# Products with v in eight 64x32 streams, maxima exchanged by ScalarE in some slots, and new tables of steps

## The chip, the cores and the metric

The kernel runs on one core of one Trainium2 chip. The metric is the time of one execution on the device, in microseconds (us), and the time given for a kernel is the median of several runs. One execution is also recorded by the hardware profiler; its trace gives the start, length and waits of single instructions.

## The reference

The reference computes a thresholded attention and then a SwiGLU block on its output. There are 8 batches, 8 heads, 576 positions and 64 values per head; the second part sees 4608 tokens of 512 values and has 1536 hidden values. All is float32.

```python
scores = scale * np.matmul(q, k.transpose(0, 1, 3, 2))
thresh = np.max(scores, axis=-1, keepdims=True) - tau
scores = np.where(scores >= thresh, scores, -1000000000.0)
scores = scores - np.max(scores, axis=-1, keepdims=True)
attn = np.exp(scores)
attn = attn / (np.sum(attn, axis=-1, keepdims=True) + 1e-09)
attn_out = np.matmul(attn, v)
x = attn_out.transpose(0, 2, 1, 3).reshape(B * S, H * D)
g = x @ w_gate
out = (g * (1.0 / (1.0 + np.exp(-g))) * (x @ w_val)) @ w_out
```

## The kernel before, in words

**Two streams of work on one TensorE.** The attention of one batch is computed while the SwiGLU block of the batch before it runs, so that TensorE always has matmuls. Batch 0's attention comes first and is written in another form (until about 142 us of the span); the text here is about what follows. Batches 1 to 7 each have four segments (one segment is a pair of heads), and each segment has five *slots*. A slot takes 128 query positions of both heads, or, in the fifth slot of a segment, the last 64. Within a batch the slots are numbered kk = 0 to 19; kk = 4, 9, 14 and 19 are the short fifth slots. Over the first two of these batches the code also counts s = 20 x (batch - 1) + kk, from 0 to 39. After batch 7 (about 1198 us) the attention is over, and only the rest of the SwiGLU block runs.

**What a slot does.** `slot_scores` (matmul on L1513) computes one or two *units* of scores. A unit is eight matmuls of shape 64x32 (64 rows of contraction, 32 output partitions), each streaming 288 columns, into a PSUM tile `sc`. There are two such tiles, used in turn, so a unit can start only when the masks of the unit before last have been computed. Then `slot_rest` makes the jobs of the other engines, in this chain:

1. VectorE takes each row's maximum, negated (L1535, tile `mx`). A query's row lies in two groups of 32 partitions, so the maxima of neighbouring groups are exchanged: `largest` does that by four small VectorE reductions across groups (L1541) and a final one (L1542, tile `nm`).
2. ScalarE computes the threshold (L1545, tile `th`) and the exponentials from PSUM into `pall` (L1549).
3. VectorE applies the mask and sums (L1550). This frees the PSUM tile.
4. ScalarE exchanges the sums of the two groups by four small copies (L1564), VectorE adds them and takes the reciprocal (L1569, L1570).
5. Each of the two or four tiles of the slot is scaled by the reciprocal: the odd tiles by GpSimd (L1577) unless the slot is in the table `BY_ACT`, the others by ScalarE (L1580). The short slots are scaled by ScalarE always.
6. VectorE transposes the slot's tiles in blocks of 32x32 (L1581).

**The products with v.** `attend` (L1600) takes a whole segment, once the transposes of all its five slots are done. It runs directly behind the scores of the second slot of the next segment (kk = 1, 6, 11, 16; the last of the 28 segments follows other work). Nine steps over blocks of keys accumulate in two PSUM banks, one for each half of the contraction rows; before the change a step is four matmuls of shape 64x64, each streaming 288 columns.

**What fills the rest of a slot on TensorE.** `block_part` puts matmuls of the SwiGLU block behind the scores. For batch 0's tokens (while batch 1's attention runs) these are plain products (`plain_group`, L1037), as many steps per slot as the table `PLAIN` says, and then output products (L1103) as `CH0` says. From batch 2's attention on they are products by a seven-product scheme with the gate and value weights (`Group`, L937; PSUM tiles `pa`, `pb`, `pe`), with steps per slot in `GV` for kk = 2 to 14; and then the products with the output weights, in one such level for the second batch of tokens (`Outputs`, L1103, table `CH`), in two levels from then on (`Deep`, L1305 and L1317, table `CD`). `CH` holds for kk = 16 to 19 and for kk = 0 and 1 of the next batch. A step of `GV` is one product of 1.73 us.

**What sets the order.** The engines run their instructions in the order in which they are written. A planner (`Plan`) chooses that order while the program is made: every job has an engine, an expected time, a rank and the jobs that it needs, and the planner simulates the engines' queues with these times. `pe(took, fn, ...)` is a TensorE step: it forces the jobs that it needs, runs the other engines' jobs up to the present planned time, and adds `took`. So the times written in the code change no instruction, but they change which of two jobs comes first on an engine.

```python
m = pe(0.655, fn, *ready, *deps, *deep_jobs[o])       # L1308, one inner product of the two-level scheme
marks.append(pe(0.7, fn, *deps, *seg["qk"]))          # L1516, one unit of scores
m = pe(4.75, fn, *seg["turned"], seg["vj"], *holds[0].deps, *holds[1].deps)   # L1603, products with v
slot_rest(seg, t, pss, marks, b > DEEP and kk in BY_ACT)   # L1766, DEEP is 2
```

By the last of these lines, batches 1 and 2 (b at most `DEEP`) scale all their odd tiles on GpSimd, and `BY_ACT` counts for batches 3 to 7 alone.

Of the kernel before, what the change touches and what calls it, by code (L numbers as in the profile page):

```python
# [14 lines left out]
ALU = mybir.AluOpType  # L15
AX = mybir.AxisListType
# [11 lines left out]
class Plan:  # L28
# [68 lines left out]
    def pe(self, took, fn, *deps):  # L97
        self.force(*deps)
        for d in deps:
            if d is not None:  # L100
                self.t = max(self.t, (d.end if isinstance(d, Job) else d) + self.HOP)
        self.run(self.t)
        fn()
        self.t += took
        return self.t + self.PIPE
# [7 lines left out]
def kernel(  # L113
# [11 lines left out]
    nc = tc.nc  # L125
    P = 128
    B, H, S, D = q.shape
# [4 lines left out]
    G = 32  # L132
    NG = P // G
# [3 lines left out]
    NK = NJ // 2  # L137
    SM = 512
    NT = SM // P
    SH = S // 2  # L140
# [421 lines left out]
    ready = deque()  # L562
# [161 lines left out]
    job, pe = plan.job, plan.pe  # L724
# [57 lines left out]
    DEEP = 2  # L782
# [422 lines left out]
    deep_jobs = [[] for _ in operands]  # L1205
# [27 lines left out]
    class Deep:  # L1233
# [60 lines left out]
        def nested(self, o, holds, first, *deps):  # L1294

            ws = weights_of(o)
            begun = set() if first else {0, 1}
            for n in self.ORDER:
                a, ready = self.inner[o][n]
                bank_, at_ = self.AT[n]  # L1300

                def fn(n=n, a=a, bank_=bank_, at_=at_):
                    ps = holds[bank_].ap()[:, at_ * P:(at_ + 1) * P]
                    for f in range(NF2 // 2):
                        nc.tensor.matmul(ps, a[:, f, :], ws[n][:, f, :], start=bank_ not in begun, stop=True, skip_group_check=True)  # L1305
                        begun.add(bank_)

                m = pe(0.655, fn, *ready, *deps, *deep_jobs[o])  # L1308
            return m

        def flat(self, o, a, hold, first, *deps):
# [206 lines left out]

    turned_jobs = {}

    def slot_rest(seg, t, pss, marks, by_act=False):
        m = 2 * len(pss)
        mx, nm, th, ri, tot = statistics("mx", "nm", "th", "ri", "tot")
        sm = sums[0]
        sums.rotate(1)
        old_sums, sum_users[0] = sum_users[0], []
        sum_users.rotate(-1)
        scs = [ps[:, h, 0:SH] for ps in pss for h in range(2)]
        base, order = seg["p"]
        first = order(t)  # L1530
        ps = [pall[:, base + (first + x) * SH:base + (first + x + 1) * SH] for x in range(m)]
        whole = pall[:, base + first * SH:base + (first + m) * SH]
        rs = []
        for x, tile_ in enumerate(pss):
            rs.append(job("DVE", 0.72, lambda x=x, tile_=tile_: nc.vector.tensor_reduce(  # L1535
                out=mx[:, 2 * x:2 * x + 2, 0], in_=tile_[:, :, 0:SH], axis=AX.X, op=ALU.max, negate=True), marks[x], rank=0))

        def largest():
            for g in range(NG):
                o = g ^ 1  # L1540
                nc.vector.tensor_reduce(out=mx[g * G:(g + 1) * G, 0:m, 1], in_=mx[o * G:(o + 1) * G, 0:m, 0:1], axis=AX.X, op=ALU.max)  # L1541
            nc.vector.tensor_reduce(out=nm[:, 0:m], in_=mx[:, 0:m, :], axis=AX.X, op=ALU.min)  # L1542

        nj = job("DVE", 0.82, largest, *rs, rank=0)
        tj = job("ACT", 0.25, lambda: nc.scalar.activation(th[:, 0:m], nm[:, 0:m], AF.Identity, bias=cut, scale=-1.0), nj, rank=0)  # L1545
        masks, users = [], [[] for _ in pss]
        ej = tj
        for x in range(m):
            ej = job("ACT", 0.42, lambda x=x: nc.scalar.activation(ps[x], scs[x], AF.Exp, bias=nm[:, x:x + 1]), ej, rank=0)  # L1549
            mj = job("DVE", 0.45, lambda x=x: nc.vector.scalar_tensor_tensor(  # L1550
                out=ps[x], in0=scs[x], scalar=th[:, x:x + 1], in1=ps[x], op0=ALU.is_ge, op1=ALU.mult, accum_out=sm[:, x, 0:1]),
                ej, *old_sums, rank=0)
            masks.append(mj)
            users[x // 2].append(mj)
        for u in users:
            sc_users[0] = u
            sc_users.rotate(-1)
        if len(users) == 1:
            pass

        def exchange():
            for g in range(NG):
                o = g ^ 1
                nc.scalar.copy(sm[g * G:(g + 1) * G, 0:m, 1], sm[o * G:(o + 1) * G, 0:m, 0])  # L1564

        xj = job("ACT", 0.78, exchange, *masks, rank=1)

        def total():
            nc.vector.tensor_reduce(out=tot[:, 0:m], in_=sm[:, 0:m, :], axis=AX.X, op=ALU.add)  # L1569
            nc.vector.reciprocal(out=ri[:, 0:m], in_=tot[:, 0:m])  # L1570

        rj = job("DVE", 0.36, total, xj, rank=1)
        sum_users[-1].append(rj)
        scaled = []
        for x in range(m):
            if x % 2 and t < NT and not by_act:
                scaled.append(job("POOL", 1.02, lambda x=x: nc.gpsimd.tensor_scalar(  # L1577
                    out=ps[x], in0=ps[x], scalar1=ri[:, x:x + 1], scalar2=None, op0=ALU.mult), rj, rank=1))
            else:
                scaled.append(job("ACT", 0.46, lambda x=x: nc.scalar.activation(ps[x], ps[x], AF.Copy, scale=ri[:, x:x + 1]), rj, rank=2))  # L1580
        seg["turned"].append(job("DVE", 0.72 * len(pss), lambda: nc.vector.transpose(out=whole, in_=whole), *scaled, rank=2 if t < NT else 1))  # L1581
# [4 lines left out]
    def attend(seg):  # L1586
        i = seg["i"]
        b, cc = divmod(i, NP)
        base, _ = seg["p"]
        p = pall[:, base:base + 2 * NK * SH].rearrange("p (k h j q) -> p h k j q", h=2, j=NK, q=G)  # L1590
        vr = seg["v"]
# [3 lines left out]
        def fn():  # L1595
            for j in range(NK):
                for a in range(R):
                    rs = slice(a * rows, (a + 1) * rows)
                    for h in range(2):
                        nc.tensor.matmul(holds[a].ap()[h * D:(h + 1) * D, 0:SH].rearrange("d (i q) -> d i q", q=G),  # L1600
                                         vr[rs, h, j, :], p[rs, h, :, j, :], start=(j == 0), stop=(j == NK - 1))

        m = pe(4.75, fn, *seg["turned"], seg["vj"], *holds[0].deps, *holds[1].deps)  # L1603
        kh, c2 = divmod(cc, 2)
        xk = x_place(b, kh)[:, :, c2, :].rearrange("p t (i a q) -> p a t i q", a=2, q=G)
        xl = xlast[:, cc, :].rearrange("p (a q) -> p a q", a=2)
# [86 lines left out]
            if not state["run"]():  # L1693
                state["run"] = None

    GV = {2: 3, 3: 4, 4: 2, 5: 5, 6: 1, 7: 3, 8: 2, 9: 3, 10: 5, 11: 2, 12: 3, 13: 3, 14: 5}
    CH = {16: 1, 17: 3, 18: 2, 19: 2, 0: 3, 1: 1}
    BY_ACT = 0, 1, 4, 5, 6, 7, 9, 11, 12, 13, 14, 15, 16, 18
    CD = {15: 2, 16: 2, 17: 1, 18: 1, 19: 1, 0: 1}
    PLAIN = {5: 2, 6: 0, 10: 2, 11: 0}  # L1700
    CH0 = {14: 1, 15: 3, 16: 0, 17: 2, 18: 2, 19: 2, 20: 3, 21: 1}

    def begin_outputs(c):
        if c < DEEP:
# [39 lines left out]
    for n, seg in enumerate(halved):  # L1744
        i = seg["i"]
        for x, t in enumerate(seg["tiles"]):
# [16 lines left out]
                prepare_v(seg, attend(halved[n - 1]))  # L1763
            if s == 1:
                prepare_v(seg)
            slot_rest(seg, t, pss, marks, b > DEEP and kk in BY_ACT)  # L1766
            if x == 0 and n + 1 < len(halved):
                prepare_next(i + 1, plan.t)
            if s == 0:
# [77 lines left out]
```

## Time and profile before

| | |
|---|---|
| median of 3 runs | 1430.06 us (1429.81 to 1431.35) |
| the profiled execution | 1431.63 us |
| its span, first to last instruction | 1429.8 us |
| mean granted TensorE clock | 0.996 |
| busy: TensorE, VectorE, ScalarE, GpSimd | 97%, 76%, 60%, 50% |
| scores L1513 | 4032 records, 160.9 us busy |
| products with v L1600 | 2016 records of 64x64, 129.9 us busy |
| exchange of maxima L1541 | 560 instructions, 148 ns each |
| exchange of sums L1564 | 560 instructions, 194 ns each |
| scaling: L1580 ScalarE, L1577 GpSimd | 390 of 530 ns, 114 of 1021 ns |

A float32 matmul is recorded as two passes, so counts of matmul records are twice the number of matmuls in the code. Busy time is the union of an engine's instructions, and it isn't their sum where they overlap, as streams in different parts of the array do. Ends of matmuls are modelled; start times are the safer reading. Idle time of an engine that isn't the bottleneck costs nothing.

### The profile page before, as it was taken

How to read it: one execution, taken by the hardware profiler on the slowest of the kernel's cores; microseconds unless marked ns; L12 is line 12 of the kernel's file. 1: busy time of each engine (PE TensorE's matmuls, PEld its weight loads, DVE VectorE, ACT ScalarE, POOL GpSimd, SP SyncE). 2: the span in 40 equal slices, each digit the busy share in tenths (PEclk: the TensorE clock that was granted, in tenths of full speed). 3: DMA queues.
4: the chain of work that ended last, by engine and by line, in shares of the span. 5: the costliest groups of instructions: out<-in, count | busy, mean ns of one | idle time of the engine just before them, and what ended most of it. 6: DMA issues, size and time to landing. Idle time of an engine off the chain costs nothing.

```text
span 1429.8 us, 32622 instructions
## 1 busy us (share of the span) xinstructions
PE 1383.1 (97%) x12126; PEld 1080.7 (76%) x12126; DVE 1083.8 (76%) x3063; ACT 863.5 (60%) x2319; POOL 721.4 (50%) x672
## 2 busy tenths in 40 slices
PE   9999899999999999999999999999999999999997
PEld 6677666766777778777787777777877788889897
DVE  7988998878778886888778876888688865355364
ACT  6887666556646766677757775777567774220220
POOL 2465769865574759533864368435933494000000
PEclk9999999999999999999999999999999999999999
DMA  7734312575413441555144523454155403424411
GB/s 172 211 113 138 70 35 79 162 209 137 107 46 125 137 108 42 163 137 138 34 151 119 137 56 133 110 138 96 39 157 157 113 25 130 154 75 140 155 52 31
DMA packets 208366, 161.91 MB, mean 113 GB/s; under 512 B 166224, under 2 KB 180560, under 8 KB 202832
## 3 DMA queue, kind: packets, MB, share of 16 engines
q1 hardware_dynamic: 204608, 159.39, 39.6%
q8 instruction: 97, 1.59, 0.5%
q10 hardware_dynamic: 3600, 0.43, 0.2%
q14 instruction: 61, 0.50, 0.1%
HBM read 138.28 MB, written 21.50 MB: 112 GB/s over the span
## 4 chain that ended last, share of the span: by engine, by line
PE 74%; DVE 14%; ACT 4%; POOL 3%; issue 2%; DMA 2%; SPq 1%; ACTq 0%; DVEq 0%; POOLq 0%
PE pb L937 15%; PE px L1305 11%; PE pa L937 10%; PE pe L937 10%; PE sc L1513 8%; PE xa L1600 6%; PE py L1317 5%; PE po L1103 4%; DVE pall L1550 3%; DVE mx L1535 3%; PE sc L937 2%; DVE pall L1581 2%; ACT pall L1549 2%; DVE mx L1541 1%; DVE pall L429 1%
## 5 line engine op out<-in xcount | busy, mean ns | idle before, releaser
L1550 DVE SCALAR_TENSOR_TENSOR pall<-sc,th,pall 128x288 f32<-128x288 f32 x504 | 234.4, 511 | 70.2 <-ACT pall L1549 69.1
L937 PE MATMUL pb<-xall,big 128*128 128x256 f32 x1032 | 247.0, 382 | 0.0
L1549 ACT ACTIVATE pall<-sc,nm 128x288 f32<-128x288 f32 x504 | 215.4, 495 | 19.0 <-DVE pall L1550 18.6
L937 PEld LDWEIGHTS pb<-xall,big 128*128 128x128 f32 x1032 | 193.0, 190 | 38.6 <-issue 5.6
L1535 DVE TENSOR_REDUCE mx<-sc 128x2 f32<-128x576 f32 x252 | 179.4, 745 | 47.4 <-PE sc L1513 46.4
L1580 ACT ACTIVATE pall<-pall,ri 128x288 f32<-128x288 f32 x390 | 183.9, 530 | 21.8 <-DVE ri L1570 20.6
L1581 DVE STREAM_TRANSPOSE pall<-pall 128x1152 f32<-128x1152 f32 (+1 forms) x140 | 175.0, 1250 | 15.5 <-ACT pall L1580 11.8
L937 PE MATMUL pa<-xall,big 128*128 128x256 f32 x752 | 180.9, 383 | 0.0
L937 PE MATMUL pe<-xall,big 128*128 128x256 f32 x752 | 179.6, 382 | 0.4 <-DVE hall L990 0.4
L1513 PE MATMUL sc<-kT,qT 64*32 64x288 f32 x4032 | 160.9, 410 | 19.6 <-DVE pall L1550 16.2
L937 PEld LDWEIGHTS pa<-xall,big 128*128 128x128 f32 x752 | 140.3, 190 | 32.0 <-ACT tmp L960 7.4
L1577 POOL TENSOR_SCALAR pall<-pall,ri 128x288 f32<-128x288 f32 x114 | 115.1, 1021 | 96.3 <-DVE ri L1570 95.8
L937 PEld LDWEIGHTS pe<-xall,big 128*128 128x128 f32 x752 | 141.3, 190 | 27.6 <-issue 5.6
L1545 ACT ACTIVATE th<-nm,cut 128x4 f32<-128x4 f32 (+1 forms) x140 | 41.4, 296 | 199.5 <-DVE nm L1542 184.5
L792 POOL TENSOR_TENSOR hall<-hall,tmp 128x512 f32<-128x512 f32 x79 | 100.4, 1272 | 85.1 <-DVE hall L990 41.4
L1600 PE MATMUL xa<-pall,vall 64*64 64x288 f32 x2016 | 129.9, 405 | 7.3 <-issue 6.4
L1564 ACT COPY sums<-sums 32x4 f32<-32x4 f32 (+1 forms) x560 | 108.4, 194 | 41.7 <-DVE pall L1550 31.5
L1513 PEld LDWEIGHTS sc<-kT,qT 64*32 64x32 f32 x4032 | 57.7, 105 | 93.8 <-issue 47.0
L1600 PEld LDWEIGHTS xa<-pall,vall 64*64 64x64 f32 x2016 | 82.9, 133 | 53.0 <-issue 10.3
L792 POOL TENSOR_TENSOR tmp<-tmp 128x512 f32<-128x512 f32 x36 | 45.9, 1276 | 91.2 <-ACT tmp L1012 91.2
L1541 DVE TENSOR_REDUCE mx<-mx 32x4 f32<-32x4 f32 (+1 forms) x560 | 83.1, 148 | 10.4
L989 ACT ACTIVATE vall<-tmp 128x512 f32<-128x512 f32 x96 | 60.4, 633 | 31.7 <-DVE tmp L1002 29.0
(221 smaller groups left out, 2367.5 us busy)
## 6 DMA issues: line engine op xcount, KB each, us to landing
big<-sums_hbm SPq DMA_DIRECT2D x42, 1024.0 KB, 5.3
big<-sums_hbm SPq DMA_DIRECT2D x48, 768.0 KB, 4.9
vall<-in_v_dram SPq DMA_DIRECT2D x112, 144.0 KB, 2.9
out_dram<-big SPq DMA_DIRECT2D x32, 256.0 KB, 2.4
qT<-in_q_dram SPq DMA_DIRECT2D x112, 72.0 KB, 4.8
kT<-in_k_dram SPq DMA_DIRECT2D x112, 72.0 KB, 2.9
wo<-in_moe_w_gate_dram SPq DMA_DIRECT2D x16, 384.0 KB, 3.8
wo<-in_moe_w_val_dram SPq DMA_DIRECT2D x16, 384.0 KB, 4.4
```

Source lines behind the costliest of these rows:

```text
L792: return lambda: nc.gpsimd.tensor_tensor(out=out, in0=a, in1=b, op=op)
L937: nc.tensor.matmul(ps[:, i], w[:, k_, i * P:(i + 1) * P], x[:, k_, :], start=first and i == k_ == 0, stop=True, skip_group_check=True)
L1305: nc.tensor.matmul(ps, a[:, f, :], ws[n][:, f, :], start=bank_ not in begun, stop=True, skip_group_check=True)
L1513: nc.tensor.matmul(ps[g * G:(g + 1) * G, h, 0:SH], qT[hs, col:col + G], kT[hs, c * SH:(c + 1) * SH], start=True, stop=True)
L1535: rs.append(job("DVE", 0.72, lambda x=x, tile_=tile_: nc.vector.tensor_reduce(out=mx[:, 2 * x:2 * x + 2, 0], in_=tile_[:, :, 0:SH], axis=A ...
L1549: ej = job("ACT", 0.42, lambda x=x: nc.scalar.activation(ps[x], scs[x], AF.Exp, bias=nm[:, x:x + 1]), ej, rank=0)
L1550: mj = job("DVE", 0.45, lambda x=x: nc.vector.scalar_tensor_tensor(out=ps[x], in0=scs[x], scalar=th[:, x:x + 1], in1=ps[x], op0=ALU.is_ge, ...
L1564: nc.scalar.copy(sm[g * G:(g + 1) * G, 0:m, 1], sm[o * G:(o + 1) * G, 0:m, 0])
L1577: scaled.append(job("POOL", 1.02, lambda x=x: nc.gpsimd.tensor_scalar(out=ps[x], in0=ps[x], scalar1=ri[:, x:x + 1], scalar2=None, op0=ALU. ...
L1580: scaled.append(job("ACT", 0.46, lambda x=x: nc.scalar.activation(ps[x], ps[x], AF.Copy, scale=ri[:, x:x + 1]), rj, rank=2))
L1581: seg["turned"].append(job("DVE", 0.72 * len(pss), lambda: nc.vector.transpose(out=whole, in_=whole), *scaled, rank=2 if t < NT else 1))
L1600: nc.tensor.matmul(holds[a].ap()[h * D:(h + 1) * D, 0:SH].rearrange("d (i q) -> d i q", q=G), vr[rs, h, j, :], p[rs, h, :, j, :], start=(j ...
```

## The change

The change has five parts.

- `attend` issues its products as eight streams of shape 64x32 in place of four of 64x64: each head's 64 values are taken in two halves. The number of columns streamed by each matmul stays 288.
- `slot_rest` gets a second way to exchange the maxima: four copies on ScalarE (`others`), followed by the final reduction on VectorE. The table `MAX_BY_ACT` names the slots of batches 3 to 7 that use it, `FIRST_MAX_BY_ACT` those of batches 1 and 2 (by s).
- Which slots scale all tiles on ScalarE changes in `BY_ACT`, and batches 1 and 2 get a table of their own, `FIRST_BY_ACT` (by s). Entries for short slots, and entries over 39, have no effect.
- The tables of TensorE's steps: `GV` moves one step from slot 9 to slot 8; `CH` redistributes the output products of one batch over slots 16 to 19, 0 and 1; `PLAIN` moves one step from slot 10 to slot 4 (a slot that isn't listed has one step up to slot 13); `CH0` loses an entry of 0.
- Two of the planner's times change: 0.655 to 0.67 and 4.75 to 4.5.

```diff
-                m = pe(0.655, fn, *ready, *deps, *deep_jobs[o])
+                m = pe(0.67, fn, *ready, *deps, *deep_jobs[o])
...
-    def slot_rest(seg, t, pss, marks, by_act=False):
+    def slot_rest(seg, t, pss, marks, by_act, max_by_act):
...
-        nj = job("DVE", 0.82, largest, *rs, rank=0)
+        def others():
+            for g in range(NG):
+                o = g ^ 1
+                nc.scalar.copy(mx[g * G:(g + 1) * G, 0:m, 1], mx[o * G:(o + 1) * G, 0:m, 0])
+
+        if max_by_act:
+            oj = job("ACT", 0.78, others, *rs, rank=0)
+            nj = job("DVE", 0.18, lambda: nc.vector.tensor_reduce(out=nm[:, 0:m], in_=mx[:, 0:m, :], axis=AX.X, op=ALU.min), oj, rank=0)
+        else:
+            nj = job("DVE", 0.82, largest, *rs, rank=0)
...
-                    for h in range(2):
-                        nc.tensor.matmul(holds[a].ap()[h * D:(h + 1) * D, 0:SH].rearrange("d (i q) -> d i q", q=G),
-                                         vr[rs, h, j, :], p[rs, h, :, j, :], start=(j == 0), stop=(j == NK - 1))
-
-        m = pe(4.75, fn, *seg["turned"], seg["vj"], *holds[0].deps, *holds[1].deps)
+                    for x in range(NG):
+                        h, ds = x // 2, slice(x % 2 * G, (x % 2 + 1) * G)
+                        nc.tensor.matmul(holds[a].ap()[x * G:(x + 1) * G, 0:SH].rearrange("d (i q) -> d i q", q=G),
+                                         vr[rs, h, j, ds], p[rs, h, :, j, :], start=(j == 0), stop=(j == NK - 1))
+
+        m = pe(4.5, fn, *seg["turned"], seg["vj"], *holds[0].deps, *holds[1].deps)
...
-    GV = {2: 3, 3: 4, 4: 2, 5: 5, 6: 1, 7: 3, 8: 2, 9: 3, 10: 5, 11: 2, 12: 3, 13: 3, 14: 5}
-    CH = {16: 1, 17: 3, 18: 2, 19: 2, 0: 3, 1: 1}
-    BY_ACT = 0, 1, 4, 5, 6, 7, 9, 11, 12, 13, 14, 15, 16, 18
+    GV = {2: 3, 3: 4, 4: 2, 5: 5, 6: 1, 7: 3, 8: 3, 9: 2, 10: 5, 11: 2, 12: 3, 13: 3, 14: 5}
+    CH = {16: 3, 17: 2, 18: 2, 19: 1, 0: 2, 1: 2}
+    BY_ACT = (0, 1, 4, 5, 9, 10, 12, 13, 14, 15, 16, 18)
+    MAX_BY_ACT = (10,)
+    FIRST_BY_ACT = (3, 6, 13, 14, 18, 19, 21, 22, 23, 25, 28, 29, 30, 31, 32, 38)
+    FIRST_MAX_BY_ACT = (0, 7, 9, 10, 23, 30, 35, 36, 40, 41)
     CD = {15: 2, 16: 2, 17: 1, 18: 1, 19: 1, 0: 1}
-    PLAIN = {5: 2, 6: 0, 10: 2, 11: 0}
-    CH0 = {14: 1, 15: 3, 16: 0, 17: 2, 18: 2, 19: 2, 20: 3, 21: 1}
+    PLAIN = {5: 2, 6: 0, 10: 1, 11: 0, 0: 1, 1: 1, 2: 1, 3: 1, 4: 2, 7: 1, 8: 1, 9: 1, 12: 1, 13: 1}
+    CH0 = {14: 1, 15: 3, 17: 2, 18: 2, 19: 2, 20: 3, 21: 1}
...
-            slot_rest(seg, t, pss, marks, b > DEEP and kk in BY_ACT)
+            at_, by_act, max_by_act = (kk, BY_ACT, MAX_BY_ACT) if b > DEEP else (s, FIRST_BY_ACT, FIRST_MAX_BY_ACT)
+            slot_rest(seg, t, pss, marks, at_ in by_act, at_ in max_by_act)
```

More of the change, by code (lines that the diff above doesn't have):

```diff
@@ L1557, in slot_rest @@
             sc_users.rotate(-1)
-        if len(users) == 1:
-            pass
         def exchange():
```

## The prediction

> **What bounds the kernel now.** I read the totals first, then the chain, then the busy time by batch, and last the order of TensorE's instructions inside one batch.
>
> ```profile
> PE 1383.1 (97%) x12126; PEld 1080.7 (76%) x12126; DVE 1083.8 (76%) x3063; ACT 863.5 (60%) x2319; POOL 721.4 (50%) x672
> ...
> PE 74%; DVE 14%; ACT 4%; POOL 3%; issue 2%; DMA 2%; SPq 1%; ACTq 0%; DVEq 0%; POOLq 0%
> ```
>
> TensorE is busy 97% of the span and carries 74% of the chain. So time can go in two ways only: TensorE's own work gets shorter, or one of its few waits goes. The busy time by stretch shows where the waits are. Each row is a stretch, its length, then the busy time of each engine.
>
> ```profile
> 142.00:274.00 132.00, 120.53 (x1187) 85.55 (x1186) 119.87 (x370) 82.40 (x245) 104.14 (x97) 0.99 0.30 74
> 274.00:430.00 156.00, 152.58 (x1369) 112.69 (x1368) 124.41 (x382) 93.33 (x273) 101.25 (x104) 1.00 0.48 132
> 430.00:586.00 156.00, 155.23 (x1465) 118.33 (x1463) 123.42 (x377) 102.96 (x289) 103.26 (x99) 1.00 0.40 115
> 586.00:739.00 153.00, 149.95 (x1460) 115.78 (x1459) 122.29 (x376) 105.33 (x297) 85.86 (x81) 1.00 0.42 113
> ```
>
> Length less PE busy is TensorE's idle time: 11.5 us in batch 1, 3.4 in batch 2, 0.8 in batch 3, 3.1 in each of batches 4 to 7. Batch 1 is also where VectorE is nearly full: 119.9 of 132 us (91%), against 80% later. All the waits of the stages that the diff touches are about 28 us.
>
> The timeline of TensorE in batch 4 shows how a slot is built (start, length, instruction, count, and idle time before it in brackets).
>
> ```profile
> 644.85 1.20 PE L1513 MATMUL sc<-kT,qT 64*32 64x288 f32 x32
> 645.98 1.99 PE L937 MATMUL pe<-xall,big 128*128 128x256 f32 x8
> ...
> 650.22 0.72 PE L1513 MATMUL sc<-kT,qT 64*32 64x288 f32 x16 [0.51 <-DVE pall L1550]
> 650.87 1.99 PE L937 MATMUL pa<-xall,big 128*128 128x256 f32 x8
> ...
> 666.21 1.20 PE L1513 MATMUL sc<-kT,qT 64*32 64x288 f32 x32
> 667.34 4.60 PE L1600 MATMUL xa<-pall,vall 64*64 64x288 f32 x72
> 671.86 1.99 PE L937 MATMUL pb<-xall,big 128*128 128x256 f32 x8
> ```
>
> Read start to next start, since ends are modelled. A scores unit alone (slot 9) takes 0.65 us, two units 1.13, the products with v 4.52. One more unit costs 0.48, so a lone block of n steps of 288 columns costs 0.16 + 0.485n: 0.65 for n=1, 1.13 for 2, 4.52 for 9. The 0.16 is paid each time the tile shape changes. It also says that eight 64x32 streams and four 64x64 streams keep the same pace of 0.485 us a step. The products gain nothing inside from more streams.
>
> **What the skill says.** The Trainium skill, "TensorEngine Tiling (Array Packing)", Key Properties, says that a change of tiling mode drains TensorE, while tiles of one mode run independently. The trace agrees: single records put 0.243 us between passes in one shape (two passes a step), 0.267 after the first pass of a block, and 0.378 from the last scores pass to the first pass of L1600. "TensorE: Matmul & The Clock Gate", The mechanism, estimates some 4 ns between starts in neighbouring tiles; here it is 6.6 ns, so eight streams start within 47 ns. The same page, Part 1, describes a clock that halves for windows of about 3.4 us after idleness. The trace has one at 165.4 to 168.8 (granted clock 0.51), right after the longest wait, 2.1 us before slot 3; it costs 8 passes of 128 ns, 1.1 us.
>
> **The change, part by part.**
>
> *Products with v as 64x32.* 72 matmul records become 144 of equal length in twice the streams; likewise the weight loads: 28 x 72 = 2016 more of each. Issue isn't short: scores issue 16 records within 0.243 us. What goes is a shape change. In 27 of 28 cases the products stand right behind two scores units of the same shape, so 1.13 + 4.52 = 5.65 becomes one block of 11 steps, 0.16 + 11 x 0.485 = 5.50. That is 0.15 us. In five cases (the first, at 186.64, and one in each of batches 4 to 7) TensorE waits in between, the drain lies under the wait, and nothing is won. 22 x 0.15 = 3.3 us; where the next scores wait anyway (after slots 11, 16, 26 of the first two batches) some is lost. I take **-3.0**. Bounds: -4.0; and on the bad side no merging, 0. That nine accumulating steps hold the pace of two isn't shown; if every pass paid the 0.267 of a first pass, 18 x 0.024 x 28 = +12.
>
> *GV: slot 8 gets three steps, slot 9 two.* The wait of 0.51 us (0.59 over the usual step) before slot 9 is for the masks of slot 8's first unit. A third product of 1.73 us in slot 8 more than covers it, in batches 3 to 7, and 1.23 us in batch 2. What is late next: slot 10's second unit, which needs slot 9's masks. Slot 9 becomes 0.65 + 2 x 1.82 (650.87 to 652.70), about 4.3 us, and slot 4, of that length already, is followed by no wait. But in VectorE's timeline slot 9's masks end 5.4 us after its start, because a transpose of 1.38 slips in while ScalarE is late; slot 10's second unit asks after 4.8. So 0 to 0.6 comes back: 5 x -0.4 = **-2.0**, and **-1.0** in batch 2. Bounds -4.1 and 0.
>
> *Maxima by ScalarE.* In 13 slots (8 in the first two batches, slot 10 in five) four reductions of 149 ns leave VectorE (0.62 us) and four copies like those of L1564 (194 ns, 0.81 together) go to ScalarE, with two hand-overs of some 0.03: the chain from scores to masks grows by 0.25, more where ScalarE is inside a long activation. Queued behind them: threshold and exps of the slot, then the masks on VectorE, then the scores two units on. In the VectorE-bound batch 1 the freed time counts: 4 x 0.62 = 2.5 at best.
>
> *Scaling.* Batch 1 and 2: 26 tiles move from GpSimd (1.02) to ScalarE (0.53); ScalarE is at 62% and 60% there. In batches 3 to 7 slots 6, 7, 11 move six tiles to GpSimd, slot 10 moves two back. GpSimd idles 9.8 us before 650.42, and the products that need these transposes come 2.0 us after the last of them (665.34 against 667.34): **0**, hidden under that slack; if it is gone, each late tile costs up to 1 us, +2 over five batches, or -0.5 where ScalarE's relief (91% busy from 646 to 656) counts.
>
> *PLAIN: one step from slot 10 to slot 4.* Slot 5's wait (1.03) goes, slot 11's start is 3.5 us earlier and meets one of about that size, as 5.9 us slots do there: 0. With the maxima and scaling I take batch 1 as **-1.5**, between -5 (VectorE's 2.5, half the chain waits, the half-clock window) and +3; the rest of batch 2 (0.44 and 1.56 us of waits near 300) as **-0.5**, between -2 and +1.
>
> *CH: outputs of one batch redistributed.* No wait stands there now (slots 35 to 41), so it can only lose. Slot 39 keeps one step, 3.4 us. The one slot of that length, slot 14, is followed by 0.85 us of wait for the second unit of the next: **+0.9**. Bounds 0 and +1.5.
>
> *Planner's costs* (0.67, 4.5): no instruction changes, only the order in which jobs are written. The trace has 0.67 and 4.52, so the order should fit no worse: 0, within 1 each way.
>
> Sum: -3.0 -2.0 -1.0 -1.5 -0.5 +0.9 = **-7.1 us**. The profiled execution took 1431.63 us (span 1429.8, 1.8 outside it); it should become 1424.5. It stands 1.6 above the median of the runs, 1430.06, so the forecast for the median is **1423.0**, own range 1417 to 1427.
>
> **Rivals.**
>
> *B: TensorE gets free and waits instead.* The masks end no earlier, so what TensorE saves turns into waits for scores. For it: the chain around slot 9 runs through VectorE and ScalarE (reductions, threshold, exps, masks). Against it: 18 of the 22 merged blocks are followed by no wait. The swap then gives 0, batch 1 gives 0, half the merging stays (-1.5), CH costs 0.9: about 1429.5. That the scores and products don't merge in fact is the same outcome: -4.1 without the -3.0, 1426, if the rest holds.
>
> *C: slower, ScalarE becomes the late link.* In the eight early slots the exchange queues behind activations of 0.6 to 0.95 us, so each chain grows by up to 0.25 + 0.95 = 1.2 us where TensorE already waits: +9.6. Slot 11 adds 1.5 (like slot 13 with one product) and slot 39 0.9; the merging and swap in batches 3 to 7 give back 5.0: +7, 1437. It decides from an average delay of (5.0 - 2.4)/8 = 0.33 us a slot. For it: the hand-overs alone are 0.25. Against: ScalarE waits 53 us for VectorE's maxima in the first two batches (40.2 + 13.0 before L1545), so mostly it is free when they come.
>
> **Numbers.** Forecast 0.60, B 0.20, C 0.20. A measurement tells about 0.2% (2.9 us) from no change. The forecast's cases lie almost all beyond that; B is mostly within it, with a share at 1426 beyond; C is mostly slower. Faster 0.62, same 0.19, slower 0.19. The range 1416.5 to 1434 takes in the forecast, B, and C up to a delay of 0.8 us; about 0.06 lies below and 0.13 above.
>
> **What would show it.** Right: L1600 as 64*32 x4032, and 5.50 us from the start of the scores to the first start after the products, in place of 5.65; no bracket before the scores of slot 9; VectorE's L1541 at 508; less idle TensorE in batch 1. Wrong: a pause of 0.38 left between scores and products, or passes of over 0.25 us inside them (first step); a new bracket before slot 10's second unit (second step); longer brackets before slots 1, 8, 10, 11, 24, 31 with ScalarE's copies as the releaser (rival C).

## The result, and the profile after

The changed kernel takes 1425.72 us (median of 11 runs, 1423.61 to 1428.83), the kernel before 1431.35 us in the same session (11 runs, 1429.51 to 1432.81). The ratio is 0.9965, with a 95% interval of 0.9955 to 0.9974: it is faster, by 5.0 us (3.7 to 6.4). Forecast were 1423.0 us and a range of 1416.5 to 1434.0. The profiled execution took 1423.61 us, its span is 1421.8 us. It is the fastest of the eleven, so the parts below add up to 8.0 us of span, where the runs are 5.0 us apart; what the slower executions lose stands in no trace. The total is near the forecast, but the parts are not: two steps were badly mis-sized, with opposite signs.

From the page of the kernel after, the totals and the shares of the chain that ended last:

```profile
PE 1383.3 (97%) x14142; PEld 1089.8 (77%) x14142; DVE 1072.7 (75%) x3011; ACT 874.9 (62%) x2377; POOL 716.5 (50%) x666
...
PE 77%; DVE 12%; ACT 5%; SPq 2%; issue 2%; DMA 1%; ACTq 0%; DVEq 0%
```

TensorE's busy time is the same as before to 0.2 us, so the 8.0 us that the span lost are idle time of TensorE. TensorE has 2016 records more, those of the finer streams; VectorE has 52 fewer, ScalarE 58 more. The answering lines of the groups (instruction, count, busy us, mean ns, then idle time before and its releaser):

```profile
L1608 PE MATMUL xa<-pall,vall 64*32 64x288 f32 x4032 | 131.3, 403 | 0.2 <-PE sc L1513 0.2
...
L1541 DVE TENSOR_REDUCE mx<-mx 32x4 f32<-32x4 f32 (+1 forms) x508 | 75.5, 149 | 9.4
```

(The products with v, L1600 before, are now on L1608. Of the lines named so far, the masks on L1550 are now L1559, the exponentials L1549 are L1558, the threshold L1545 is L1554, the transposes L1581 are L1588.) The busy time by stretch, the stretches being batches 1 to 4 of this kernel (stretch, length, busy time of TensorE, its weight loads, VectorE, ScalarE and GpSimd, granted clock, DMA share, GB/s):

```profile
142.00:278.00 136.00, 123.37 (x1396) 87.50 (x1392) 116.72 (x353) 87.14 (x268) 105.04 (x97) 0.95 0.29 81
278.00:431.00 153.00, 151.71 (x1664) 113.48 (x1656) 120.41 (x359) 102.81 (x301) 75.42 (x78) 1.00 0.45 124
431.00:588.00 157.00, 155.70 (x1768) 121.41 (x1771) 123.78 (x379) 104.22 (x300) 106.68 (x102) 1.00 0.41 117
588.00:738.00 150.00, 148.98 (x1746) 115.92 (x1738) 120.69 (x370) 103.77 (x297) 89.89 (x85) 1.00 0.41 114
```

Batch 1 got longer, with 12.6 us of idle TensorE and a mean clock of 0.95 (0.99 before). Batches 2 and 4 got shorter. The lengths from the first scores of each batch to those of the next (for b7, to its last scores), in us, for this kernel and for the experiments that follow:

| kernel | until b1 | b1 | b2 | b3 | b4 | b5 | b6 | b7 | after b7 | span |
|---|---|---|---|---|---|---|---|---|---|---|
| before | 142.7 | 131.7 | 156.1 | 156.0 | 153.1 | 153.1 | 153.1 | 147.6 | 236.5 | 1429.8 |
| **after** | 141.1 | 136.6 | 153.2 | 156.7 | 150.4 | 150.5 | 150.5 | 144.9 | 238.0 | 1421.8 |
| e1_times | 140.6 | 131.7 | 158.9 | 156.0 | 150.8 | 150.8 | 150.8 | 145.2 | 237.2 | 1421.9 |
| e2_streams | 142.7 | 131.3 | 155.8 | 155.5 | 152.8 | 152.8 | 152.8 | 147.3 | 236.7 | 1427.6 |
| e3_old_times | 142.1 | 135.5 | 157.1 | 156.8 | 152.7 | 152.8 | 153.3 | 147.2 | 237.3 | 1434.9 |
| e4_max0 | 141.2 | 133.4 | 153.5 | 161.6 | 150.4 | 150.4 | 150.5 | 144.9 | 238.6 | 1424.5 |
| e5_order | 140.9 | 131.6 | 156.1 | 156.0 | 151.3 | 151.3 | 151.3 | 145.8 | 236.4 | 1420.8 |
| e6_lag8 | 141.2 | 131.3 | 153.6 | 156.7 | 150.4 | 150.5 | 150.6 | 144.9 | 238.0 | 1417.1 |
| e7_gv_old | 142.9 | 136.8 | 154.2 | 157.0 | 150.8 | 150.8 | 150.8 | 145.3 | 237.9 | 1426.4 |
| e8_four_streams | 142.0 | 138.6 | 153.6 | 157.1 | 150.7 | 150.7 | 150.7 | 145.2 | 237.5 | 1426.1 |
| e9_ch_old | 141.2 | 131.5 | 153.9 | 155.8 | 150.4 | 150.5 | 150.5 | 144.9 | 238.4 | 1416.9 |
| e10_first_old | 141.3 | 131.4 | 161.0 | 160.4 | 150.4 | 150.5 | 150.5 | 144.9 | 238.5 | 1428.8 |
| e11_sum | 141.9 | 131.3 | 156.6 | 159.8 | 151.0 | 155.2 | 156.5 | 149.7 | 237.4 | 1439.4 |
| e12_first_old_4s | 141.1 | 131.4 | 161.2 | 157.0 | 150.7 | 150.7 | 150.7 | 145.2 | 237.2 | 1425.2 |

The span went from 1429.8 to 1421.8 as +4.9 (b1), -2.9 (b2), +0.7 (b3), -10.7 (b4 to b7), +1.5 (after b7) and -1.6 (until b1). The last is no work of the change: it is a stretch of halved clock near 70 us (69.9 to 73.3 in the profile before) that some executions show and others don't. Without it the change gained 6.4 us in these two profiles.

**Where batches 4 to 7 gained.** VectorE's timeline at the end of slot 19 and the start of batch 4, first of the kernel before (start, length, instruction, count):

```profile
592.89 1.65 DVE L795 TENSOR_TENSOR big<-big,px 128x256 f32<-128x256 f32 x4
594.46 0.77 DVE L1581 STREAM_TRANSPOSE pall<-pall 128x576 f32<-128x576 f32 x1
```

and of the kernel after:

```profile
593.56 0.78 DVE L1588 STREAM_TRANSPOSE pall<-pall 128x576 f32<-128x576 f32 x1
594.26 0.38 DVE L795 TENSOR_TENSOR big<-big,px 128x256 f32<-128x256 f32 x1
```

The transpose of the short slot 19 is the last thing that the products in slot 1 need. Before, four additions of the SwiGLU block (1.65 us) stood ahead of it. What this does on TensorE, before:

```profile
592.44 1.30 PE L1513 MATMUL sc<-kT,qT 64*32 64x288 f32 x32
595.33 4.83 PE L1600 MATMUL xa<-pall,vall 64*64 64x288 f32 x72 [1.59 <-issue]
```

and after:

```profile
593.60 1.20 PE L1513 MATMUL sc<-kT,qT 64*32 64x288 f32 x32
594.59 4.57 PE L1608 MATMUL xa<-pall,vall 64*32 64x288 f32 x144
```

From scores to products it was 2.89 us and is 0.99, once per batch. The releaser in the bracket says only "issue"; it is VectorE's row that shows what was late. Nothing in the edited tables touches these instructions.

**Where batch 1 lost.** ScalarE's timeline of the kernel after, behind the scores of slot 2:

```profile
157.46 0.81 ACT L1571 COPY sums<-sums 32x4 f32<-32x4 f32 x4 [0.31 <-DVE pall L1559]
161.93 0.89 ACT L817 ACTIVATE wo<-xall 128x768 f32<-128x768 f32 x1 [3.65 <-DMA xall<-in_moe_w_out_dram]
162.73 0.96 ACT L820 ACTIVATE big<-xall,minus 128x768 f32<-128x768 uint32 x1
163.60 0.28 ACT L1554 ACTIVATE th<-nm,cut 128x4 f32<-128x4 f32 x1
```

L817 splits a piece of the output weights. It stands at the head of ScalarE's queue and waits 3.65 us for its DMA, while the threshold of slot 2, whose maxima were there at 160.5 us, stands behind it until 163.60. TensorE's row at the next scores:

```profile
165.79 2.17 PE L1513 MATMUL sc<-kT,qT 64*32 64x288 f32 x32 [3.56 <-DVE pall L1559]
```

The wait is 3.56 us, and 6.8 us of halved clock go with it, from 164.5 on. Batch 1 of this profile has two more such windows, of 3.4 us each, at 150.9 and 198.7. The first did not make it long: e7_gv_old (below), with the same tables for batch 1, has none there, waits 4.89 us in place of 3.56 for the same L817, and its batch 1 takes 136.8 us. In the kernel before this L817 ran at 169.29, behind slot 3's exponentials.

### The profile page after: what moved, and what is told of

The parts are those of the page before. It is cut to its first block, busy times and chain, and to the rows that moved or that the text cites. A ratio compares the mean times of both kernels' runs of the same rounds, so it can differ in the third digit from the quotient of the medians.

```text
span 1421.8 us, 36646 instructions
## 1 busy us (share of the span) xinstructions
PE 1383.3 (97%) x14142; PEld 1089.8 (77%) x14142; DVE 1072.7 (75%) x3011; ACT 874.9 (62%) x2377; POOL 716.5 (50%) x666
## 4 chain that ended last, share of the span: by engine, by line
PE 77%; DVE 12%; ACT 5%; SPq 2%; issue 2%; DMA 1%; ACTq 0%; DVEq 0%
PE pb L937 16%; PE pe L937 11%; PE pa L937 10%; PE px L1305 10%; PE sc L1513 9%; PE xa L1608 7%; PE py L1317 4%; PE po L1103 4%; DVE pall L1559 3%; PE sc L937 2%; DVE mx L1535 2%; ACT pall L1558 2%; DVE pall L1588 1%; DVE mx L1541 1%; SPq L334 1%
## 5 line engine op out<-in xcount | busy, mean ns | idle before, releaser
L1559 DVE SCALAR_TENSOR_TENSOR pall<-sc,th,pall 128x288 f32<-128x288 f32 x504 | 233.2, 510 | 71.6 <-ACT pall L1558 70.8
L1558 ACT ACTIVATE pall<-sc,nm 128x288 f32<-128x288 f32 x504 | 214.3, 495 | 16.7 <-DVE pall L1559 16.6
L1588 DVE STREAM_TRANSPOSE pall<-pall 128x1152 f32<-128x1152 f32 (+1 forms) x140 | 174.9, 1251 | 15.0 <-ACT pall L1587 14.3
L1584 POOL TENSOR_SCALAR pall<-pall,ri 128x288 f32<-128x288 f32 x108 | 108.1, 1014 | 106.8 <-DVE ri L1577 106.8
L1554 ACT ACTIVATE th<-nm,cut 128x4 f32<-128x4 f32 (+1 forms) x140 | 41.3, 295 | 178.7 <-DVE nm L1542 166.1
L1608 PE MATMUL xa<-pall,vall 64*32 64x288 f32 x4032 | 131.3, 403 | 0.2 <-PE sc L1513 0.2
L1608 PEld LDWEIGHTS xa<-pall,vall 64*32 64x32 f32 x4032 | 90.5, 107 | 35.4 <-DVE hall L990 1.7
L1541 DVE TENSOR_REDUCE mx<-mx 32x4 f32<-32x4 f32 (+1 forms) x508 | 75.5, 149 | 9.4
```

The lines of the kernel that those rows point to most:

```text
L1608: nc.tensor.matmul(holds[a].ap()[x * G:(x + 1) * G, 0:SH].rearrange("d (i q) -> d i q", q=G), vr[rs, h, j, ds], p[rs, h, :, j, :], start=( ...
```

## The experiments

Every kernel was timed in five rounds beside the kernel before; times are medians.

**The planner's times alone, and all but them.** e1_times is the kernel before with

```diff
-                m = pe(0.655, fn, *ready, *deps, *deep_jobs[o])
+                m = pe(0.67, fn, *ready, *deps, *deep_jobs[o])
-        m = pe(4.75, fn, *seg["turned"], seg["vj"], *holds[0].deps, *holds[1].deps)
+        m = pe(4.5, fn, *seg["turned"], seg["vj"], *holds[0].deps, *holds[1].deps)
```

> Kernel before with the two planner times alone changed (0.67 and 4.5); every instruction is the same, only the order in which they are written differs. Theory 1: the short slot's transpose (kk = 19) is now written before the four VectorE additions of the two-level scheme, so the products of kk = 1 no longer wait 1.6 us, in four batches; 2.0 us each, about 8 us in all: 1423, ratio 0.994 to 0.996. Theory 2: the times don't matter, the new tables and streams made the gain: within 1.5 us of before.

Measured: 1425.65 us, ratio 0.9962 (0.9949 to 0.9975). Theory 1 holds: two numbers that change no instruction give as much as the whole change. Batches 4 to 7 become 2.3 us shorter each; batch 2 becomes 2.8 us longer. e3_old_times is the reverse, the kernel after with 0.655 and 4.75.

> Kernel after with the old planner times (0.655 and 4.75). Theory 1: the transpose of kk = 19 goes back behind the additions, the four waits of 1.6 us return, and it is 8 us slower than after: 1433, ratio to before 1.001 to 1.003. Theory 2: as after, 1425.

Measured: 1439.61 us, ratio 1.0061 (1.0045 to 1.0077). The direction is theory 1's, the size more: 13.9 us slower than after. The wait of 1.59 us ahead of the products of slot 1 is back (at 600.49 in its timeline), and batch 2 loses 3.9 us. The rest of the change, planned with the old times, is slower than no change.

**The order itself.** e5_order leaves the times alone and lifts one rank, for slot 19 of batches 3 to 7 (in the trace the order then differs in batches 4 to 7 alone):

```diff
-        seg["turned"].append(job("DVE", 0.72 * len(pss), lambda: nc.vector.transpose(out=whole, in_=whole), *scaled, rank=2 if t < NT else 1))
+        seg["turned"].append(job("DVE", 0.72 * len(pss), lambda: nc.vector.transpose(out=whole, in_=whole), *scaled, rank=2 if t < NT else 0 if seg["i"] % NP == NP - 1 and seg["i"] // NP > DEEP else 1))
```

> The kernel before, with its own planner's times and its four streams; only the rank of the transpose of each batch's last short slot (kk = 19, batches 3 to 7) is raised, so that it stands ahead of the four VectorE additions of L795. Theory 1: the gain from the planner's times is this one order; the wait of 1.59 us ahead of the products of kk = 1 goes in batches 4 to 7, about 2 us each, batch 2 keeps its 156.1 us: 1422.5, ratio 0.994. Theory 2: the gain comes from the other changes of order that the new times bring: within 2 us of before.

Measured: 1422.62 us, ratio 0.9946 (0.9934 to 0.9958), as theory 1 gave. TensorE's timeline of this kernel at the same place:

```profile
590.60 1.30 PE L1513 MATMUL sc<-kT,qT 64*32 64x288 f32 x32
591.83 4.76 PE L1600 MATMUL xa<-pall,vall 64*64 64x288 f32 x72
597.12 0.72 PE L1513 MATMUL sc<-kT,qT 64*32 64x288 f32 x16 [0.53 <-DVE pall L1550]
```

The wait ahead of the products is gone; 0.53 us come back behind them, since the next scores now ask early for slot 1's masks. From the scores of slot 1 to the first product of slot 2 it is 8.39 us, against 9.68 before: 1.3 us of the 1.8 that each of batches 4 to 7 gains. The other 0.5 comes further on, and wasn't traced to one instruction; the rank is one edit, but the planner answers it with nine changes in VectorE's order and nine in ScalarE's in each of these batches. Batch 2 keeps its length. One rank is worth at least as much as the whole change: 7.2 us by these batches, 7.7 (6.0 to 9.4) by the ratio.

**The streams.** e2_streams is the kernel before with the new loop of `attend` alone; e8_four_streams is the kernel after with the old one (shown is the latter):

```diff
-                    for x in range(NG):
-                        h, ds = x // 2, slice(x % 2 * G, (x % 2 + 1) * G)
-                        nc.tensor.matmul(holds[a].ap()[x * G:(x + 1) * G, 0:SH].rearrange("d (i q) -> d i q", q=G),
-                                         vr[rs, h, j, ds], p[rs, h, :, j, :], start=(j == 0), stop=(j == NK - 1))
+                    for h in range(2):
+                        nc.tensor.matmul(holds[a].ap()[h * D:(h + 1) * D, 0:SH].rearrange("d (i q) -> d i q", q=G),
+                                         vr[rs, h, j, :], p[rs, h, :, j, :], start=(j == 0), stop=(j == NK - 1))
```

> Kernel before with the products with v as eight 64x32 streams alone, old planner times, so the order of all jobs is that of before. Theory 1: 22 blocks of scores and products merge at 0.16 us each, 3.5 us: 1427.5, ratio 0.9975; the waits of kk = 1 stay. Theory 2: the merging is taken back by later waits: ratio above 0.999. If nine steps in eight streams ran slower, ratio above 1.005.

> The kernel after with the products in four 64x64 streams, all else kept. Theory 1: the merged block is worth 0.16 us in 22 of 28 cases less what moves into waits, so this is 1 to 3 us slower than after: 1427 to 1429. Theory 2: 288 TensorE instructions within 4.4 us at times outrun the fetch of instructions, which takes the gain back: no slower than after, and its runs lie closer together (the runs of after spread over 5 us).

Measured: e2_streams 1429.66 us, ratio 0.9992 (0.9984 to 1.0000), a gain of 1.1 us (0 to 2.3). Theory 1's 0.9975 lies outside that interval; by the ratio it is theory 2. e8_four_streams 1426.03 us, ratio 0.9969 (0.9957 to 0.9981): against after's 0.9965 no difference can be told, which is theory 2's number, but its runs spread over 3.2 us and the profile of after shows no lack of instructions, so its reason isn't shown there. In the profiles the size is easier to see. In e2_streams batches 1 to 7 are 2.6 us shorter in sum, and the 28 blocks of scores and products alone 2.5 us; in e8_four_streams batches 2 to 7 are 1.9 us longer. So the streams are worth about 2 us in the profiled executions, and 0 to 2.3 in the runs. TensorE's timeline of after shows the merged block as forecast, and a case that gains nothing:

```profile
629.53 1.20 PE L1513 MATMUL sc<-kT,qT 64*32 64x288 f32 x32
630.52 4.57 PE L1608 MATMUL xa<-pall,vall 64*32 64x288 f32 x144
635.02 1.99 PE L937 MATMUL pb<-xall,big 128*128 128x256 f32 x8
...
664.59 1.20 PE L1513 MATMUL sc<-kT,qT 64*32 64x288 f32 x32
665.58 4.89 PE L1608 MATMUL xa<-pall,vall 64*32 64x288 f32 x144
670.40 1.99 PE L937 MATMUL pb<-xall,big 128*128 128x256 f32 x8
```

From scores to what follows the products it is 635.02 - 629.53 = 5.49 us in slot 6, but 5.81 in slot 11, against 5.66 before in both. Slot 11's is no price of the streams: with four of them and all else kept (e8_four_streams) it is 5.84 there and 5.66 in slot 6. So it comes with the rest of the change, and not with the streams.

**The table GV.** e7_gv_old is the kernel after with slots 8 and 9 as before.

```diff
-    GV = {2: 3, 3: 4, 4: 2, 5: 5, 6: 1, 7: 3, 8: 3, 9: 2, 10: 5, 11: 2, 12: 3, 13: 3, 14: 5}
+    GV = {2: 3, 3: 4, 4: 2, 5: 5, 6: 1, 7: 3, 8: 2, 9: 3, 10: 5, 11: 2, 12: 3, 13: 3, 14: 5}
```

> The kernel after with the old table GV (two steps in slot 8, three in slot 9). Theory 1 (as predicted): the swap gives 0.4 us in each of batches 3 to 7 and 1 us in batch 2, so this is 3 us slower than after: 1428.7. Theory 2 (rival B in this place): the wait only moved to slots 10 and 11, and only batch 2 gains: 1 to 1.3 us slower than after, about 1427.

Measured: 1427.77 us, ratio 0.9979 (0.9972 to 0.9986), 2.05 us slower than after by the medians, which lies between the theories' 3.0 and 1.3. By the batches batch 2 loses 1.0 us and batches 3 to 7 lose 0.2 to 0.4 each, 1.6 in sum. In each place that is theory 1, a little smaller. The wait ahead of slot 9 is 0.95 us in this kernel (before 652.59) and none in after, where slot 10's second unit waits instead (from 654.26, 1.56 us for two units, where 1.20 is usual).

**Batch 1.** e4_max0 takes slot 0 out of the table of maxima; e6_lag8 leaves every table alone and tells the planner that the fetch ahead of L817 takes longer:

```diff
-    FIRST_MAX_BY_ACT = (0, 7, 9, 10, 23, 30, 35, 36, 40, 41)
+    FIRST_MAX_BY_ACT = (7, 9, 10, 23, 30, 35, 36, 40, 41)
```

```diff
-                j = job("SP", 0.1, fetch, done.get(place), lag=5.0)
+                j = job("SP", 0.1, fetch, done.get(place), lag=8.0)
```

> Kernel after with slot 0 taken out of FIRST_MAX_BY_ACT. Theory 1: the exchange of maxima itself costs little; its side effect is that a part of the weight split (L817) is written on ScalarE ahead of slot 2's exponentials and waits there for a DMA for 3.65 us, after which TensorE's clock halves. With slot 0's maxima on VectorE the split goes back behind slot 3's exponentials: 4 to 5.5 us faster than after, 1420 to 1422, ratio 0.992 to 0.994. Theory 2: batch 1 is long because the exchanges in slots 7, 9 and 10 and the scaling lengthen the chain; then it is less than 1 us faster than after.

> The kernel after, where the planner is told that a fetch of output weights takes 8 us in place of 5. Only the places of two ScalarE instructions (L817 and L820 on the tile xall) and the order of a few on VectorE change, all in batch 1. Theory 1: batch 1 lost 5 us because L817 stood at the head of ScalarE's queue and waited 3.65 us for its DMA, with slot 2's threshold and exponentials behind it: batch 1 becomes 132 to 133.5 us (136.6 now), the time 1421 to 1422.5. Theory 2: the exchange by ScalarE and the scaling there are what makes batch 1 long: less than 1 us faster than after.

Measured: e4_max0 1425.8 us, ratio 0.9958 (0.9946 to 0.9970), no gain by the median. Its batch 1 is 3.2 us shorter, since L817 moved to 167.78, but its profiled batch 3 is 4.9 us longer: TensorE stopped for 2.77 us within the products of slot 1 (from 436.45), which is taken up below. Whether the other runs stopped there isn't known. e6_lag8 took 1421.14 us, ratio 0.9938 (0.9924 to 0.9953). ScalarE's timeline of e6_lag8:

```profile
159.38 0.30 ACT L1554 ACTIVATE th<-nm,cut 128x4 f32<-128x4 f32 x1 [1.99 <-DVE nm L1542]
...
164.10 0.90 ACT L817 ACTIVATE wo<-xall 128x768 f32<-128x768 f32 x1
```

The threshold no longer waits for a DMA, batch 1 takes 131.3 us, and no halved clock is left in it. Moving two instructions of ScalarE (VectorE swaps two of its own as well, at 173 to 179 us) is worth 5.3 us in batch 1, of which batch 2 gives 0.4 back: theory 1. The exchange of maxima by ScalarE and the scaling in it are not what made batch 1 long.

**The tables of the first two batches.** e9_ch_old and e10_first_old start from e6_lag8. e9_ch_old changes

```diff
-    CH = {16: 3, 17: 2, 18: 2, 19: 1, 0: 2, 1: 2}
+    CH = {16: 1, 17: 3, 18: 2, 19: 2, 0: 3, 1: 1}
```

and e10_first_old, with the new CH,

```diff
-    FIRST_BY_ACT = (3, 6, 13, 14, 18, 19, 21, 22, 23, 25, 28, 29, 30, 31, 32, 38)
-    FIRST_MAX_BY_ACT = (0, 7, 9, 10, 23, 30, 35, 36, 40, 41)
+    FIRST_BY_ACT = ()
+    FIRST_MAX_BY_ACT = ()
...
-    PLAIN = {5: 2, 6: 0, 10: 1, 11: 0, 0: 1, 1: 1, 2: 1, 3: 1, 4: 2, 7: 1, 8: 1, 9: 1, 12: 1, 13: 1}
+    PLAIN = {5: 2, 6: 0, 10: 2, 11: 0}
```

> The kernel of e6_lag8 with the old table CH besides (outputs of one batch of tokens, slots 16 to 19 of batch 2 and 0 and 1 of batch 3). Theory 1 (as predicted, +0.9 for the new table): batch 3 goes from 156.7 back to 156.0 us, the time from 1421.1 to 1420.3. Theory 2: the short slot 39 only moves a wait, and the sum of batches 2 and 3 stays within 0.3 us: 1421.

> The kernel of e6_lag8 with the tables of the first two batches as before: no maxima by ScalarE there, scaling of odd tiles on GpSimd there, PLAIN and CH0 old. Theory 1 (from the traces): those tables bring batch 1 nothing (131.3 us either way) and batch 2 about 1.5 us: 1422.6. Theory 2 (as predicted): 1.5 us in batch 1, where VectorE is the nearly full engine, and 0.5 in batch 2: 1423.1, with batch 1 at 132.8 and batch 2 at 154.1.

Measured: e9_ch_old 1418.86 us, ratio 0.9916 (0.9903 to 0.9928), the fastest of all and faster than both kernels. In the profiles batch 3 is 0.9 us shorter than in e6_lag8, as forecast for CH, with 0.3 given back in batch 2 and 0.4 after batch 7. The medians differ by 2.3 us and their intervals touch, so between 0.2 and 2.3 the worth of the old CH stays open. e10_first_old took 1429.72 us, ratio 0.9986 (0.9978 to 0.9995): both theories missed. Batch 1 is the same (131.4), so the tables bring nothing there, which is theory 1. But batch 2 is 7.4 us longer, with waits of 1.8 us at 334.90 (for L944) and 2.6 us at 350.25 (for L990) that neither kernel has: the old tables under the new times give another plan. And batch 3 is 3.8 us longer for another reason:

```profile
440.94 1.20 PE L1513 MATMUL sc<-kT,qT 64*32 64x288 f32 x32
441.94 3.26 PE L1608 MATMUL xa<-pall,vall 64*32 64x288 f32 x95
448.46 1.88 PE L1608 MATMUL xa<-pall,vall 64*32 64x288 f32 x49 [3.27 <-issue]
```

TensorE stands still for 3.27 us in the middle of a block whose operands are all there. In the trace its instructions come as DMA packets of 16 KB on queue 8 (97 in before, 113 in after). I counted the records of matmuls and weight loads from the start of one packet to the start of the next: it is about 250 on average, and 170 to 340 in more than nine cases of ten. Here the packet started at 446.0 us, after 470 of them, and TensorE went on 2.5 us later. In e4_max0 it is 469 and 2.4 us. In the other twelve profiles the count never goes over 396, and none has such a stop. So TensorE had most likely none left; the trace doesn't say so itself.

**Do finer streams cause that stop?** e12_first_old_4s is e10_first_old with four 64x64 streams; no other engine's order differs.

> The kernel of e10_first_old with the products in four 64x64 streams; no other engine's order changes. In e10_first_old TensorE stood still for 3.4 us inside the products at 444.8 us, while its next instructions arrived late behind 1.8 MB of weights. Theory 1: with half as many instructions in the block TensorE does not run out of them; batch 3 goes from 160.4 to about 157 us (4.7 less, 0.4 back for the shape changes, clock window included), the time from 1429.7 to about 1427, with 3 us more lost in the other batches as in e8_four_streams: 1427 to 1429, and no stop inside a block. Theory 2: the late arrival stops TensorE in any form of the products: the stop stays, and the time rises by 2 to 3 us.

Measured: 1426.35 us, ratio 0.9965 (0.9953 to 0.9977), 3.4 us faster than with eight streams. Batch 3 takes 157.0 us, theory 1's number, and TensorE's timeline has no gap:

```profile
440.98 1.20 PE L1513 MATMUL sc<-kT,qT 64*32 64x288 f32 x32
442.11 4.60 PE L1607 MATMUL xa<-pall,vall 64*64 64x288 f32 x72
446.63 5.45 PE L1103 MATMUL po<-wo,hall 128*128 128x256 f32 x24
```

The block of nine steps takes 288 records in 4.5 us with eight streams, and 144 with four, so it uses up a packet in half the time. Why the packet came late is open. My expectation named the weights ahead of it, and the DMA view of e10_first_old (40 equal slices from 436 to 448 us, busy tenths of the DMA engines) speaks against that:

```profile
DMA  2696000000000000000090567799999999979510
...
q8 instruction: 1, 0.02, 0.5%
```

The DMA engines were idle from 437.2 to about 442 us, while the count since the last packet went from some 180 to 300, and the packet didn't come then. Nor does e12_first_old_4s settle it wholly: with fewer records its packets end at other places of the program.

**Adding up what gained.** e11_sum takes the three clearest edits together: e5_order with the new loop of `attend` and the new GV.

```diff
-    GV = {2: 3, 3: 4, 4: 2, 5: 5, 6: 1, 7: 3, 8: 2, 9: 3, 10: 5, 11: 2, 12: 3, 13: 3, 14: 5}
+    GV = {2: 3, 3: 4, 4: 2, 5: 5, 6: 1, 7: 3, 8: 3, 9: 2, 10: 5, 11: 2, 12: 3, 13: 3, 14: 5}
...
-                    for h in range(2):
+                    for x in range(NG):
+                        h, ds = x // 2, slice(x % 2 * G, (x % 2 + 1) * G)
...
```

> The kernel of e5_order with the eight streams and the new table GV; every other table and the planner's times as before. Theory 1: the gains add up, since each stands at another place: 1422.6 less 2.6 for GV (what e7_gv_old shows in its batches) less 1 to 2 for the streams: 1418 to 1419, the fastest so far. Theory 2: each edit reorders the other engines and so undoes part of the others: 1421 or more.

Measured: 1438.81 us, ratio 1.0048 (1.0035 to 1.0061), 16 us slower than e5_order. Theory 2 in direction, far beyond it in size. TensorE's timeline of e11_sum in batch 3:

```profile
497.32 0.71 PE L1513 MATMUL sc<-kT,qT 64*32 64x288 f32 x16
497.97 1.99 PE L937 MATMUL pb<-xall,big 128*128 128x256 f32 x8
503.05 3.65 PE L937 MATMUL pe<-xall,big 128*128 128x256 f32 x8 [3.08 <-DVE hall L990]
```

and VectorE's there:

```profile
502.04 0.16 DVE L1569 TENSOR_REDUCE tot<-sums 128x4 f32<-128x12 f32 x1
502.24 0.18 DVE L1570 RECIPROCAL ri<-tot 128x4 f32<-128x4 f32 x1
502.33 0.66 DVE L990 SCALAR_TENSOR_TENSOR hall<-vall,pb 128x512 f32<-128x512 f32 x1
```

The second product of slot 9 waits until L990 has read the tile `pb`, most likely because it was given the PSUM bank that `pb` held (the trace leaves out which). Which bank a new product takes is the planner's choice too (`take`, by the time at which it expects each to be free), and L990 came late behind slot 9's masks. The wait of over 3 us stands in batches 3, 5, 6 and 7, with halved clock behind it. Which of the two added edits tips it wasn't run.

## Why the prediction was right or wrong

| step | forecast, us | measured |
|---|---|---|
| products as 64x32, a shape change less | -3.0 | e2_streams -1.1 (0 to -2.3) by ratio; -2.6 (e2_streams) and -1.9 (e8_four_streams) by the batches |
| GV in slots 8 and 9 | -3.0 | -2.05 by the median of e7_gv_old, -2.6 by its batches |
| maxima, scaling, PLAIN in batch 1 | -1.5 | +4.9 in after; -0.3 once L817 is out of the way |
| the rest of batch 2 | -0.5 | -1.5, what is left of -2.9 after GV and streams; the planner's new times are in it |
| CH | +0.9 | +0.2 to +2.3 |
| planner's costs | 0, within 1 | -5.2 alone (e1_times), -13.9 within the change (e3_old_times) |

**The planner's costs are the failed step.** The prediction argued that with 0.67 and 4.52 in the trace "the order should fit no worse". That bounded the wrong thing. The size of a planner's time is no measure of its effect: a change of 0.25 us decides which of two ready jobs goes first, and in slot 19 that was a transpose with TensorE behind it against four additions with slack. The page before had shown the wait (the prediction counted it, "one in each of batches 4 to 7", as a place where merging wins nothing), but it took the wait as given and did not ask which VectorE instruction ended it. Two rows further that was to be read.

**Batch 1 is the second.** The step counted VectorE's freed time and the longer chain, and the places queued behind the new copies. It did not ask what else the planner would move when slot 0's copies shift ScalarE's plan: a weight split that waits for a DMA. Rival C named ScalarE as the late link in the early slots, and in slot 3 it was; but behind a DMA at the head of its queue, not behind an activation under way, and in one slot, not in eight. The halved clock that the prediction cited from the Trainium skill, "TensorE: Matmul & The Clock Gate", Part 1, came with it: 6.8 us with a wait of 3.56 us, none in batch 1 of e6_lag8. The page names an idle window of about 3.4 us as what brings it; in the trace before it stood behind a wait of 2.10 us. The prediction also priced that window too low, at 1.1 us: the block of 16 records in it (L1037 at 165.38) took 5.41 us, where 3.72 is usual, so 1.7.

**What held.** The working 0.16 + 0.485n holds for the merged block: 5.50 us for eleven steps. It was over-sized because not every block could use it: in slot 11 it won 0.03 (5.84 us with four streams, 5.81 with eight), and in slot 1 what follows the products, the next scores, came 6.06 us after the first scores with four streams and with eight (rival B, in these places). GV did what was said, with the return at slot 10's second unit that was named as late next. CH cost about what was said in batch 3. VectorE's relief from the maxima and the scaling moved no end of batch 1, though VectorE was 91% busy there: with e10_first_old against e6_lag8 it is 131.4 against 131.3 us. The price of eight streams that was not in the prediction is the stop for instructions, some 3 us when it comes. The prediction had said "Issue isn't short", from 16 records within 0.243 us; that is the pace of records that are at hand, and says nothing of when the next ones are fetched.

**The signs cancel.** -5 or more that was not forecast, +6.4 against forecast in batch 1, and the rest near: that is why 1425.7 lies near 1423.0. The range held for the wrong reasons as much as for the right ones.

## What to carry to other kernels

Where a planner or a hand-written order decides which of two ready instructions goes first, treat each of its numbers as an edit of every queue: write the program with and without the edit and compare the order engine by engine, then look for the instruction that a wait on the bottleneck engine ends on. A wait whose bracket says only "issue" is still worth following to the other engines' rows at that time; here one rank, given to put one transpose ahead of four additions, gained 7.7 us (6.0 to 9.4), no less than the change's five parts together. And gains measured one by one in such a kernel don't add up: of the three edits of e11_sum one gained 7.7 us alone, one about 1 us alone and one about 2 us within the change, and together they lost 7.4 us, so the combination itself has to be run (here e9_ch_old, 1418.86 us, ratio 0.9916).

## What the runs showed of the hardware

- TensorE can stand still with all its operands ready, most likely for want of instructions. In two of the profiled kernels with eight streams it stopped for 2.77 and 3.27 us inside a block, and went on 2.4 and 2.5 us after its next 16 KB packet of instructions had started; 469 and 470 records had been issued since the packet before, where no profile without a stop goes over 396. The second of these programs, with half as many and larger matmuls in the block, didn't stop. A matmul is one record however small its tile, so the finest tiling has a cost that busy times don't show.
- A DMA at the head of an in-order queue costs what stands behind it: 3.65 us on ScalarE, with one 768 KB transfer that takes about 5.4 us from issue to landing.
- A wait of 3.56 us on TensorE went with 6.8 us at half clock. Shorter waits don't decide it: one of 2.10 us in before was followed by 3.4 us of it, and the wait of 1.67 us ahead of slot 1 of batch 1 by 3.4 us in after and by none in e6_lag8 and e7_gv_old.
